# Three edits around the raw loads of a fused RWKV-7 and mixture kernel: R first, loads ahead of the placement, products on GpSimd

## The chip, the cores and the metric

The kernel runs on one core of a Trainium2 chip. The metric is the device time in microseconds (us) of one execution; before the change the median of three runs is 1277.89 us. TensorE multiplies matrices, VectorE (DVE in the profile) and ScalarE (ACT)[...], GpSimd (POOL) works in SBUF, and SyncE (SP) issues most of the DMAs.

## The reference, cut to what matters

Two blocks follow each other. The first is a recurrence with a state matrix for each batch and head (4 batches, 8 heads, 768 steps, 40 columns):

```python
for t in range(S):
    y[:, :, t] = einsum('bhd,bhde->bhe', r_t, state)
    Sa = einsum('bhde,bhe->bhd', state, a_t)
    state = state * w_t - einsum('bhd,bhe->bhde', Sa, b_t) + einsum('bhd,bhe->bhde', v_t, k_t)
```

Its output, laid out as x with 3072 rows of 320, goes through four experts, each 320 to 1024 to 320 columns, weighted by normalized probabilities:

```python
p = domain_probs / (domain_probs.sum(-1) + 1e-9)
for e in range(4):
    out += p[:, e] * (maximum(x @ w1[e], 0) @ w2[e])
```

## The kernel before

The recurrence is cut into chunks of 64 steps. A unit is one chunk of a pair of batches, so there are 24 units, two for each of the 12 chunks. For a unit the kernel does four things.

- `within(q)` works without the state. It loads raw w, transposes it by channels into G and makes G the running product of the decays (a scan); rG is its reciprocal. A, B, K, V and R come as raw tiles from HBM (rawA and so on, one buffer each), are transposed 32 by 32 on VectorE (L229) and become AT, NT, KT, VT and RT. AT is multiplied by G, NT and KT by rG: these are the decay products (L423). A first group of matmuls, pc, multiplies RT with VT; a second, pfe, multiplies AT with NT and KT and gives F (copied by ScalarE) and ET.
- `substitute(q, eng)` inverts the triangular matrix in F. VectorE prepares M (L529 to L545); from the third unit on, GpSimd then computes Z from M by 16 steps of three instructions each (L554, L567).
- `merge(q)` transposes Z on VectorE into Qc and QTc (L578, L580), GpSimd copies QTc into QT (L586), and the matmuls pY and pQ complete QT.
- `step(q, xT)` carries the state: matmuls prn, psat, pxr and pdy with evictions on ScalarE and VectorE (EV, SN, SaT, SX, RS), then Y and the new state. From the third chunk on, twelve DMAs on the SyncE queue place Y into xT (L718, "the placement").

The experts run on the xT of a finished chunk as pieces in a list, `todo`. The product with w2 uses a Strassen-like scheme: `up` multiplies by w1 into two banks ph (L733, L741), ScalarE applies relu into hs, VectorE forms the sums a1, a7, a5, a2, a6 of hs (L842), `down_1` computes p431, `down_2` p75 and p26 (L848), and VectorE adds them to osb (L757, L759). The weights w1 stream through two buffers (w1p); ph, p431, p75 and p26 share three PSUM buffers of the tag "mm".

The main loop takes one unit u in an iteration and weaves stages of four units: the step of u, the merge of u+1, `within` and `substitute` of u+2 and the first loads of u+3. Generators are advanced by `run(gen, n)`; `gap(n)` lets `mix` put in one or two mixture pieces. The raw loads of u+3 are not issued at once but kept in the list `later`; `begin_later(n)` issues the next n of them after each piece, and the rest at once in the next iteration:

```python
        run(s)
        ...
        begin_later(len(later))
        run(w, 1)
        if not early:
            run(m, 1)
        gap(1)
```

Here the third `run(s)` issues the placement of Y, `run(w, 1)` transposes A, B, K, V and R and forms the products, and the first `run(m, 1)` of the merge transposes Z into Qc and QTc. In the early iterations (u below 5) the merge stands elsewhere.

A scheduler turns this program into one fixed order for each engine. `tc.keep_in_program_order` pins an instruction; the loads of `begin_later`, the transposes of M and of Z and the QT copies are pinned, the decay products of later units and the placement are not. Each engine works through its own queue in the resulting order and waits at semaphores.

Of the kernel before, what the change touches and what calls it, by code (L numbers as in the profile page):

```python
# [9 lines left out]
ALU = mybir.AluOpType  # L10
# [5 lines left out]
def kernel(  # L16
# [38 lines left out]
    nc = tc.nc  # L55
# [16 lines left out]
    def big(name):  # L72
# [6 lines left out]
        out=ident[:], in_=ident[:], pattern=[[1, P]], compare_op=ALU.is_equal, fill=0.0,  # L79
# [5 lines left out]
    for t, n, op in ((upf, L, ALU.is_gt), (diagf, Q, ALU.is_equal)):  # L85
        nc.vector.memset(t[:], 1.0)
        for q in range(P // n):
            o = slice(q * n, (q + 1) * n)
            nc.gpsimd.affine_select(
                out=t[o], in_=t[o], pattern=[[1, n]], compare_op=op, fill=0.0, base=0, channel_multiplier=-1,  # L90
# [63 lines left out]
    PADDED = 3  # L154
# [21 lines left out]
    units = []  # L176

    def begin(u):
        q = Unit()
        q.u, q.c, q.bp = u, u // (B // 2), u % (B // 2)  # L180
        q.b = [2 * q.bp, 2 * q.bp + 1]
        q.start, q.end = q.c == 0, q.c == NC - 1
        q.n = {}
        units.append(q)
        return q

    def load(q, names):
        for x in names:
            q.n[x] = t = sb.tile([P, H, D], FP32, name=f"nat{x}", tag=f"nat{x}", bufs=2 if x == "V" else 1)
            for i, bb in enumerate(q.b):  # L190
                nc.sync.dma_start(
                    out=t[i * L:(i + 1) * L], in_=srcs[x][bb, :, q.c * L:(q.c + 1) * L, :].rearrange("h t e -> t h e"),
                )

    def load_raw(q, names):


        moves = []
        for x in names:
            q.n["raw" + x] = t = raw[x]()  # L200
            heads = srcs[x].rearrange("b h t e -> (b h) t e")[q.b[0] * H:(q.b[1] + 1) * H, q.c * L:(q.c + 1) * L, :]
            heads = heads.rearrange("n (x two) e -> x n (two e)", two=2)
            for r in range(2):
                hs = slice(r, 16, 2)
                for y, los, w_ in ((0, (0,), D + Q), (1, (0, D) if x == "W" else (0,), D - Q if x == "W" else 2 * D - Q)):
                    o = slice(64 * r + Q * y, 64 * r + Q * y + Q)
                    for lo in los:
                        cols = slice(Q * y + lo, Q * y + lo + w_)
                        moves.append(
                            lambda eng, out=t[o, :, lo:lo + w_], in_=heads[:, hs, cols]: eng.dma_start(out=out, in_=in_)  # L210
                        )
        return moves
# [10 lines left out]
    def go(moves, eng=None):  # L223
        for move in moves:
            move(eng or nc.sync)

    def turn_raw(out, t):

        return nc.vector.transpose(  # L229
            out=out.rearrange("p n (x two) -> p n two x", two=2),  # L230
            in_=bass.AP(t.tensor, t.offset, [list(t.ap[0]), list(t.ap[1]), [D, 2], [1, Q]]),
        )
# [152 lines left out]
    def within(q):  # L385

        n = q.n

        def pin(ins, also=False):
            if q.u <= PADDED or also:  # L390
                tc.keep_in_program_order(ins)
# [5 lines left out]
        for i in range(2):  # L397
# [5 lines left out]
            out=G[:, 0:2 * NJ * L], data0=G[:, 0:2 * NJ * L],  # L403
# [5 lines left out]
        def turn_padded(x):  # L409
            return turn(f"p{x}T", tok(padded[min(q.u, 1)][x]), q.u == 1)[:].rearrange("p (j i t) -> p j i t", i=2, t=L)  # L410

        def by_channels(name, buf, n_bufs, x, factor=None):

            t = sb.tile([P, 2 * NJ, L], FP32, name=name, tag=buf, bufs=n_bufs)
            to = t[:].rearrange("p (i j) t -> p j i t", i=2)
            if q.u < PADDED:
                src = turn_padded(x)
            else:
                pin(turn_raw(t[:], n["raw" + x][:]))
                src = to  # L420
            if factor is not None:
                factor = factor.rearrange("p (j i) t -> p j i t", i=2)
                pin(nc.vector.tensor_tensor(out=to, in0=src, in1=factor, op=ALU.mult))  # L423
            elif q.u < PADDED:
                nc.scalar.copy(out=to, in_=src)
            return t
# [146 lines left out]
    def merge(q):  # L573


        Qc = sb.tile([P, H, Q], FP32, name="Qc", tag="q", bufs=2)
        QTc = sb.tile([P, H, Q], FP32, name="QTc", tag="q", bufs=2)
        tc.keep_in_program_order(nc.vector.transpose(out=dealt(Qc[:]), in_=q.Z))  # L578
        tc.keep_in_program_order(
            nc.vector.transpose(  # L580
                out=QTc[:].rearrange("p h r -> p (h r)"), in_=Qc[:].rearrange("p h c -> p (h c)"),
            )
        )
        q.QT = QTs()
        for i in range(P // Q):
            ins = nc.gpsimd.tensor_copy(out=q.QT[quarter(i), :, quarter(i % 2)], in_=QTc[quarter(i)])  # L586
            tc.keep_in_program_order(ins)
        yield

        py = big("pY")  # L590
        for h in range(H):
            for i in (1, 3):
                nc.tensor.matmul(
                    out=py[quarter(i - 1), h * Q:(h + 1) * Q], lhsT=q.F[quarter(i), h, 0:Q],
                    rhs=QTc[quarter(i), h, :], start=True, stop=True,
                )
        Y = sb.tile([P, H, Q], FP32, name="Yq")
        for i in (0, 2):
            nc.scalar.copy(out=Y[quarter(i)].rearrange("p h t -> p (h t)"), in_=py[quarter(i), 0:H * Q])
        yield  # L600

        pq = big("pQ")
        for h in range(H):
            for i in (0, 2):
                nc.tensor.matmul(  # L605
                    out=pq[quarter(i), h * Q:(h + 1) * Q], lhsT=Qc[quarter(i), h, :],
                    rhs=Y[quarter(i), h, :], start=True, stop=True,
                )
        for i in (0, 2):
            nc.scalar.copy(out=q.QT[quarter(i), :, quarter(1)], in_=by(pq[quarter(i), 0:H * Q], Q))  # L610
        yield
# [296 lines left out]
    todo, last, later = [], [], []  # L908

    def begin_later(n):  # L910
        for move in later[:n]:
            tc.keep_in_program_order(move(nc.sync))
        del later[:n]

    def mix(n):

        for piece in todo[:n]:
            piece()
            begin_later(3 if n > 1 else 6)
        del todo[:n]  # L920

    def run(gen, n=99):
        if gen is None:
            return
        for _ in range(n):
            if next(gen, gen) is gen:
                break
# [3 lines left out]
    def begin_step(u):  # L931
        q = units[u]
        if q.bp == 0:
            chunks_x[q.c] = sb.tile([P, 3, 2 * P], FP32, name="xT", tag="xT", bufs=2)
        q.xT = chunks_x[q.c][:, :, q.bp * P:(q.bp + 1) * P]
        return step(q, q.xT)
# [79 lines left out]
    for u in range(1, NU):  # L1016
        q = units[u]
        m = s_next = w = w_next = iter(())
        if u + 1 < NU:
            m, s_next = merge(units[u + 1]), begin_step(u + 1)  # L1020
            w_next = ws[u + 1]
        if u + 2 < NU:
            w = ws[u + 2]

        def gap(n, pieces=None):
            at = 4 * u + n
            run(sum_ops, sums_at.get(at, 0))
            mix((1 if at in sparse else 2) if pieces is None else pieces)

        run(w, 1)  # L1030
        run(w_next)
        run(s, 1)
        gap(0)


        early = u < 5
        run(s, 1)
        run(w, 1)
        run(s)
        if u == 1:  # L1040
            mixture_of_unit(q)
        elif q.bp:
            mixture_of_chunk(units[u - 1:u + 1], chunks_x[q.c])
        begin_later(len(later))
        run(w, 1)
        if not early:
            run(m, 1)
        gap(1)

        if u + 3 < NU:  # L1050
            go(load_raw(begin(u + 3), "W"))
            load(units[u + 3], "BKV")
            later.extend(load_raw(units[u + 3], "BAKVR"))
        run(w, 1)
        if early:
            run(m, 1)
        else:
            run(s_next, 1)
            run(m, 1)
        gap(2)  # L1060
# [5 lines that stand above are left out]
            run(s_next, 1)  # L1066
        if u + 2 < NU:
            substitute(units[u + 2], nc.gpsimd)
        run(w, 1)
        if u + 3 < NU:  # L1070
            ws.append(within(units[u + 3]))
            run(ws[u + 3], 1)
        if early:
            run(m, 1)
            run(s_next, 1)
            run(m)
            gap(3, 1)
            run(s_next, 1)
            mix(0 if 4 * u + 3 in sparse else 1)
        else:  # L1080
            gap(3)
        s = s_next
# [31 lines left out]
```

## Time and profile before

| | |
|---|---|
| runs | 1277.89 us median, 1271.62 to 1294.58 |
| profiled span | 1283.8 us |
| granted TensorE clock, mean | 0.887 |
| VectorE decay products L423 of later units | 21 each of AT, NT, KT; 688, 723, 711 ns |
| GpSimd per unit, steady part | 48 instructions of Z, 4 QT copies, 1 copy into Z |
| SyncE placement | 12 issues a unit, 8.9 us |

In the profile a line of the timeline gives start, duration, engine, line, operation, output and inputs, count, and in brackets how long the engine had been idle before it and what released it. A line of waits gives the waiting instruction, the one it waited for, the total, how often and the longest. PEclk shows the granted clock of TensorE in tenths over 40 slices of the span.

### The profile page before, as it was taken

To read this page: it belongs to the slowest core of one execution; us is meant where nothing else is said; L and a number is where in the kernel's file an instruction comes from. 1 tells how busy PE (TensorE), PEld (TensorE's weight loads), DVE (VectorE), ACT (ScalarE), POOL (GpSimd) and SP (SyncE) were. 2 spreads that over 40 slices of the span, in tenths; PEclk is the share of its full clock that TensorE was granted. 3 is DMA by queue.
4 is the path that set the end of the run, shared out by engine and by line. 5 is a ranking of instruction groups with operands and counts; after the bars stand their busy time and mean duration, and the time that the engine had idled before them with its cause. 6 is when DMAs were issued, how large, how long until landed. Compare 5 with 4: busy or idle time off the path is not lost.

```text
span 1283.8 us, 38036 instructions
## 1 busy us (share of the span) xinstructions
PE 1200.6 (94%) x15828; PEld 1045.6 (81%) x15828; DVE 829.7 (65%) x1642; ACT 331.1 (26%) x844; POOL 475.2 (37%) x1226
## 2 busy tenths in 40 slices
PE   5889988999999999999989999999999999999998
PEld 4767766888788888888878888888888887888887
DVE  7865576789656756676566666676666766644334
ACT  2222333223223122232231322322213323122110
POOL 4024555464253351552524515425244253350000
PEclk7789987999797887997979899789797997899999
DMA  7657642445334424443343443442434334212221
GB/s 147 141 135 196 137 91 67 98 101 125 84 99 100 105 74 99 95 114 85 84 109 85 108 104 87 104 99 72 107 86 112 86 104 89 84 57 86 86 76 31
DMA packets 299491, 126.73 MB, mean 99 GB/s; under 512 B 244360, under 2 KB 272696, under 8 KB 299320
## 3 DMA queue, kind: packets, MB, share of 16 engines
q1 hardware_dynamic: 296312, 123.84, 40.5%
q8 instruction: 125, 2.05, 0.7%
q10 hardware_dynamic: 3008, 0.46, 0.2%
q14 instruction: 46, 0.38, 0.1%
HBM read 116.36 MB, written 3.93 MB: 94 GB/s over the span
## 4 chain that ended last, share of the span: by engine, by line
PE 75%; DVE 10%; SPq 7%; DMA 5%; issue 2%; ACT 1%; DVEq 0%; ACTq 0%
PE ph L741 25%; PE p L848 20%; PE ph L733 9%; SPq L718 3%; PE pfe L374 3%; PE pdy L374 2%; PE psat L374 2%; PE prn L374 2%; DMA w1p<-in_moe_w_dram 2%; PE po L782 2%; SPq L210 2%; PE pxr L374 2%; PE pQ L605 2%; DVE osb L759 2%; PE pc L374 1%
## 5 line engine op out<-in xcount | busy, mean ns | idle before, releaser
L741 PE MATMUL ph<-xT,w1p 128*128 128x256 f32 (+1 forms) x1520 | 370.1, 400 | 0.0
L741 PEld LDWEIGHTS ph<-xT,w1p 128*128 128x128 f32 x1520 | 293.3, 203 | 74.6 <-issue 26.3
L567 POOL TENSOR_TENSOR Z<-Z 128x31 f32<-128x31 f32 (+7 forms) x704 | 256.9, 365 | 55.2
L554 POOL TENSOR_TENSOR Z<-M,Z 128x62 f32<-128x62 f32 (+7 forms) x352 | 156.0, 443 | 294.9 <-DVE M L545 258.6
L842 DVE TENSOR_TENSOR a<-hs 128x512 f32<-128x512 f32 x220 | 152.5, 710 | 145.6 <-ACT hs L746 145.6
L746 ACT ACTIVATE hs<-ph 128x512 f32<-128x512 f32 (+1 forms) x208 | 117.2, 564 | 439.9 <-PE ph L741 439.6
L759 DVE SCALAR_TENSOR_TENSOR osb<-p,gate,osb 128x320 f32<-128x320 f32 (+1 forms) x243 | 108.1, 480 | 128.6 <-PE p L848 125.1
L848 PE MATMUL p<-sums,a 128*128 128x160 f32 x1056 | 164.8, 299 | 0.0
L586 POOL COPY QT<-QTc 32x256 f32<-32x256 f32 x96 | 40.1, 418 | 326.7 <-DVE QTc L580 309.1
L848 PEld LDWEIGHTS p<-sums,a 128*128 128x128 f32 x1056 | 152.9, 190 | 2.2
L733 PE MATMUL ph<-xT,w1p 64*128 64x256 f32 (+1 forms) x760 | 138.1, 442 | 0.6 <-ACT xT L710 0.6
L848 PE MATMUL p<-w,hs 128*128 128x160 f32 x704 | 104.2, 301 | 0.0
L848 PE MATMUL p<-w,a 128*128 128x160 f32 x704 | 102.8, 299 | 0.0
L848 PEld LDWEIGHTS p<-w,hs 128*128 128x128 f32 x704 | 100.8, 191 | 2.3
L848 PEld LDWEIGHTS p<-w,a 128*128 128x128 f32 x704 | 98.0, 190 | 0.0
L733 PEld LDWEIGHTS ph<-xT,w1p 64*128 64x128 f32 x760 | 79.5, 207 | 20.1 <-issue 6.3
L439 DVE RECIPROCAL rG<-G 128x504 f32<-128x504 f32 x24 | 79.1, 3296 | 0.0
L634 ACT COPY SN<-prn 64x256 f32<-64x256 f32 x88 | 32.2, 366 | 159.0 <-DVE EV L630 156.6
L529 DVE STREAM_TRANSPOSE M<-blocks 128x1024 f32<-128x1024 f32 x24 | 46.3, 1931 | 35.4 <-ACT blocks L526 35.1
L374 PE MATMUL pc<-RT,VT 40*64 40x64 f32 x768 | 21.2, 264 | 40.4 <-DVE RT L229 39.0
L374 PEld LDWEIGHTS pc<-RT,VT 40*64 40x64 f32 x768 | 17.3, 168 | 46.7 <-DVE RT L229 43.6
L374 PE MATMUL pdy<-VC,k_tok 64*64 64x104 f32 (+1 forms) x768 | 43.6, 269 | 0.0
(153 smaller groups left out, 1489.7 us busy)
## 6 DMA issues: line engine op xcount, KB each, us to landing
w1p<-in_moe_w_dram SPq DMA_DIRECT2D x95, 512.0 KB
w1p<-in_moe_w_dram SPq DMA_DIRECT2D x190, 64.0 KB
w<-in_moe_w_dram SPq DMA_DIRECT2D x4, 1280.0 KB
sums<-in_moe_w_dram SPq DMA_DIRECT2D x9, 512.0 KB
out_dram<-osb SPq DMA_DIRECT2D x46, 80.0 KB
rawW<-in_w_dram SPq DMA_DIRECT2D x47, 72.0 KB
natB<-in_b_dram SPq DMA_DIRECT2D x42, 80.0 KB
natK<-in_k_dram SPq DMA_DIRECT2D x42, 80.0 KB
```

Of the source, the lines that this page charges most:

```text
L374: nc.tensor.matmul(out=p[row][half(col), lo + at * out_cols:lo + (at + 1) * out_cols], lhsT=lhsT, rhs=rhs, start=(n == 0), stop=(n == len( ...
L439: pin(nc.vector.reciprocal(out=rG[:, :, 0:L - 1], in_=Gv[:, :, 1:L]))
L529: ins = nc.vector.transpose(out=M[:], in_=cols)
L554: ins = eng.tensor_tensor(out=Z[:, 1:3, 0:n, j + 1:Q], in0=M[:, j:j + 2, None, j + 1:Q].to_broadcast([P, 2, n, m]), in1=Z[:, here, 0:n, j: ...
L567: eng.tensor_tensor(out=z[:, 0], in0=z[:, 0], in1=z[:, x], op=ALU.add)
L586: ins = nc.gpsimd.tensor_copy(out=q.QT[quarter(i), :, quarter(i % 2)], in_=QTc[quarter(i)])
L733: nc.tensor.matmul(out=ph[i][:, f, :], lhsT=w1.last[i * DT:(i + 1) * DT, f, :], rhs=xT[i * DT:(i + 1) * DT, 2, :], start=(f == 0), stop=False,
L741: nc.tensor.matmul(out=ph[i][:, f, :], lhsT=w1.main[:, g, at * P:(at + 1) * P], rhs=xT[:, g, :], start=False, stop=(g == 1 and f == HF // ...
L746: nc.scalar.activation(out=h[:, i * HF // 2:(i + 1) * HF // 2, 0:n], in_=ph[i][:], func=ACTF.Relu,)
L759: nc.vector.scalar_tensor_tensor(out=to, in0=p, scalar=sc, in1=to, op0=ALU.mult, op1=ALU.add)
L842: nc.vector.tensor_tensor(out=t[:], in0=x, in1=y, op=op)
L848: nc.tensor.matmul(out=p[:, n * HD:(n + 1) * HD], lhsT=a[:, f, :], rhs=b[:, f, :], start=(f == 0), stop=(f == HF - 1),)
```

## The change

It has three parts. The raw loads of a unit come in the order R, B, A, K, V, four for each piece of mixture instead of three, and the remainder is issued before the step's last stages, hence before the placement of Y, so that R isn't the last to arrive. The products of A, B and K with the decays go to GpSimd for every unit from the fourth on. And the order of the later iterations begins at u = 4 instead of 5.

```diff
-                pin(nc.vector.tensor_tensor(out=to, in0=src, in1=factor, op=ALU.mult))
+                pin((nc.vector if q.u < PADDED else nc.gpsimd).tensor_tensor(out=to, in0=src, in1=factor, op=ALU.mult))
...
-            begin_later(3 if n > 1 else 6)
+            begin_later(4 if n > 1 else 6)
...
-        early = u < 5
+        early = u < 4
         run(s, 1)
         run(w, 1)
+        begin_later(len(later))
         run(s)
         if u == 1:
             mixture_of_unit(q)
         elif q.bp:
             mixture_of_chunk(units[u - 1:u + 1], chunks_x[q.c])
-        begin_later(len(later))
         run(w, 1)
...
-            later.extend(load_raw(units[u + 3], "BAKVR"))
+            later.extend(load_raw(units[u + 3], "RBAKV"))
```

## The prediction

> **What bounds the kernel now.** I read the busy shares first, then the list of who waited for whom on TensorE, then the timelines of a steady unit, then the clock in stretches.
>
> ```profile
> PE 1200.6 (94%) x15828; PEld 1045.6 (81%) x15828; DVE 829.7 (65%) x1642; ACT 331.1 (26%) x844; POOL 475.2 (37%) x1226
>
> PE pc L374 <- DVE RT L229: 39.0, 18, 3.2
> PE pev L374 <- DVE ET L381: 13.0, 3, 6.2
> 545.00 0.70 DVE L229 STREAM_TRANSPOSE RT<-rawR 128x512 f32<-128x512 f32 x1
> 545.76 1.09 PE L374 MATMUL pc<-RT,VT 40*64 40x64 f32 x32 [2.16 <-DVE RT L229]
> 538.03 0.97 SPq L210 DMA_DIRECT2D rawR<-in_r_dram  x2
> ```
>
> TensorE is the bound. Its one repeated idle gap is 2.16 us before pc, waiting for RT: R's last two raw loads stand on SyncE behind twelve xT placements (8.93 us) and RT is transposed late on VectorE. The clock pays more than the gap:
>
> ```profile
> 281.68:286.00 4.32, 4.32 (x138) 3.98 (x139) 4.29 (x9) 0.73 (x2) 3.03 (x5) 1.00 0.54 159
> 493.70:498.75 5.05, 5.05 (x135) 4.04 (x136) 4.31 (x11) 2.19 (x6) 1.97 (x5) 0.60 0.67 107
> ```
>
> The columns are stretch, length, busy time of PE, PEld, DVE, ACT, POOL, then granted clock. After the 1.20 us gap at 281.68 the clock stayed 1.00; after the 2.16 us gaps it fell to 0.50. In stretches of 1 us the low episodes last 4 to 18 us, most of them 14 to 18, and lose 7.06 us of clock per unit on average.
>
> A unit of the steady part, from the end of pfe to the end of the next, at full clock and without gaps, from rows at clock 1.00: psat 1.0; four ph blocks of 4.71 (L733 1.06, L741 3.65), 18.84; two p431 of 3.26, 6.52; two p75 with p26 of 4.35, 8.70; pev 0.6, pxr 0.95, pdy 1.74, pg 0.59, pc 0.55, prn 1.05, pY 0.62, pQ 0.62, pfe 1.0. Sum 42.8. With the gap 2.16 and the clock 7.06: 52.0. From pc at 387.95 to pc at 1115.52 are 14 units of 51.97. So the account closes.
>
> GpSimd solves one unit's triangular system, Z:
>
> ```profile
> 510.76 0.29 POOL L554 TENSOR_TENSOR Z<-M,Z 128x62 f32<-128x62 f32 x1 [13.82 <-DVE M L545]
> 532.50 0.52 POOL L567 TENSOR_TENSOR Z<-Z 128x8 f32<-128x8 f32 x2
> 545.63 0.58 DVE L578 STREAM_TRANSPOSE Qc<-Z 128x256 f32<-128x256 f32 x1
> 1152.05 0.63 DVE L578 STREAM_TRANSPOSE Qc<-Z 128x256 f32<-128x256 f32 x1 [3.52 <-POOL Z L567]
> ```
>
> Z takes 22.3 us from M (L545); its only reader, Qc, comes 12.6 us after it ended, so it's hidden. Only in the last unit does Qc stand near: VectorE then sat 3.52 us. This is the wait to watch.
>
> **What the Trainium skill says.** "TensorE: Matmul & The Clock Gate", Part 1: idling drops the array to half clock, and sustained work of some 3.4 us lifts it. The 0.50 agrees; but here 2.16 us of idling beside small matmuls is enough, and once dense work is back (503.95) it takes 5 us. The same page, under the array's architectural detail: VectorE's queue is strict FIFO. The 3.52 us agree: everything behind Qc waited too. "GPSIMD Engine Reference", section 3.1: a two-input tensor_tensor of 2048 elements takes 4497 ns. No 128x512 product on GpSimd is in this trace; this gives 1.12 us for 512, an estimate. L554's fastest, 0.23 us at 16 elements and 0.45 at 152, extrapolate to 1.03; section 8's sharing of SBUF interfaces with VectorE shows as L567 going from 217 to 1246 ns. I take 1.2 and bound it at 1.0 and 2.0.
>
> **The change part by part.**
> Products to GpSimd: 63 of them leave VectorE (15.2 + 14.4 + 14.9 = 44.5 us, 2.1 a unit). They add 3 x 1.2 = 3.6 us a unit to GpSimd (2.0 each: 6), behind Z and ahead of the QT copies, where it idles 13.81 us. Readers are pfe for NT and KT, prn for AT. Hidden, both ends.
> R first, raw loads ahead of the placement, four loads in place of three a piece: the same DMAs. R lands early, the 2.16 us gap closes. V becomes last but no longer waits for 8.93 us of placement issues.
> Later order one unit sooner: iteration 4 alone, about nothing.
>
> What the diff doesn't show is where these put Qc. In the order of the changed program, VectorE's queue has, in every second unit (call it E):
>
> ```
> L545 M<-M,Z          (Z may start)
> L759 osb<-p431 x4
> L381 SX<-pxr x2
> L229 RT<-rawR
> L578 Qc<-Z           (waits for all of Z)
> L580 QTc<-Qc
> L842 a1, a7;  L759 osb<-p75;  L842 a5;  L759 osb<-p75
> ```
>
> Qc is 8 rows after M; in the kernel before 46. In the other units (O) it is 22 rows after. E and O alternate from the eighth to the 23rd unit: eight pairs. Queued behind Qc are a1, a7 and the osb additions that read p75; the second ph bank of the next up-projection waits on TensorE for exactly the last of these, since it takes p75's PSUM buffer.
>
> Unit E, clock zero at the end of pfe. VectorE: F at 0.8, ET 0.43, blocks 0.57, ET 0.40, G's four instructions and scan 2.5 (4.8); M transposed 1.93, gl 0.17, the reciprocal 3.3, which now stands ahead, 0.17, then 0.69 + 0.69: M ends at 11.8. Z: 0.35 to start, and 19.5 to run (fastest of every form and its gaps add up to 18.9; VectorE, idle, disturbs little): 31.7. Qc 0.6, QTc 0.45, a1 and a7 1.4, osb 0.55, a5 0.68, osb 0.37: 35.9. TensorE: psat 1.0, ph 4.7, p431 3.26, pev and pxr 1.55, ph 4.7, p75 and p26 4.35, pdy and pg 2.3: at 22.0 it's out of work. **Stall 13.9 us.** Later pc waits for VT, behind the next a1, barely; then VectorE reaches VC and EV late, SN and Yq on ScalarE follow (1.5 + 0.75), and pQ stands 2.2 us.
>
> Unit O: M ends near 6.8 (the reciprocal now after it), Z at 28.7 with contention. Here p75's buffer is free at 25.3, so Qc costs TensorE some 0.8. But pg needs rG, at 14.7, where TensorE is free at 10.6: 4.1 us.
>
> Clock: the old episode at pc goes with its gap. In E the restart after 13.9 us costs about 3 (half of the 5 to 7 us for which dense work ran slow before), the stand at pQ perhaps 3; in O the stand at pg about 3.
>
> E: 42.8 + 13.9 + 2.2 + 6 = 64.9. O: 42.8 + 4.1 + 0.8 + 3 = 50.7. A pair 115.6 against 103.9: +11.7, eight pairs +93. Units six and seven (Qc 13 and 17 rows after M) and iteration 4 gain the gap and part of the clock and lose some of it at Qc: -5. 1278 + 93 - 5 = **1366 us**.
>
> **The rivals.**
> A, faster: Qc doesn't hold VectorE up, and gap and clock episode go. For it: the 2.16 us gap is aimed at precisely, and the unit after 281.68 ran at 1.00 throughout. Full effect 18 x (2.16 + 7.06) = 166, 1112 us; with the clock falling at the small matmuls anyway, 18 x 2.16, 1239. Against: the 22 us of Z don't fit into the 3.1 us of VectorE work (osb 1.6, SX 0.78, RT 0.7) between M and Qc.
> B, stall but little clock loss: only 3 us of slow clock in a pair, no stand at pQ: pair 42.8 x 2 + 13.9 + 4.9 + 3 = 107.4, +28 over eight, 1301 us. If TensorE's stand were 4 us shorter too, nearly no change. For it: no episode has been seen after a stall amid dense work.
> C, stall with long episodes: 7 us more at pQ and at pg as at pc before, 3 at the restart: pair 123.7, +158, 1431. For it: pQ and pg stand beside the same small matmuls as pc did.
> D, GpSimd becomes the bound: 22 + 6 + 2 us of a unit of 50 is not enough.
>
> **How the numbers follow.** Forecast 0.55, B 0.17, C 0.17, A 0.08, D 0.03 (near 1400). A is almost all faster; a third of B is within 2%. So faster 0.06, same 0.05, slower 0.89. The range reaches from B to just short of C: 1300 to 1420.
>
> **What would show it.** Right: VectorE idle on Qc waiting for POOL Z for about 16 us in every second unit from the eighth on (some 130 us in all); TensorE's ph L733 waiting for VectorE osb for about 14 us as often; the RT wait before pc gone; PE busy under 90%; L423 on POOL between 1.0 and 2.0 us. Wrong: Qc following Z without idle time, units below 52 us, or pc waiting for VT as long as it did for RT.

## The result, and the profile after

The changed kernel takes 1341.75 us (median of three runs, 1341.01 to 1345.63), against 1277.89 before. All ratios here are taken against the kernel before timed beside each run, and leave out the executions that ran in a slower state, so they differ a little from the ratio of two medians. This one is 1.053 with a 95% interval of 1.046 to 1.061: 5.3% slower. The profiled span is 1343.8 us against 1283.8, the mean granted clock 0.907 against 0.887. So the profiled execution is 60 us longer although TensorE's mean clock got better.

First the page of the changed kernel: the busy shares, the engines' shares of the chain that ended last, and two groups of instructions (count, then busy time and mean ns of one, then the idle time of the engine just before them and who ended most of it).

```profile
PE 1156.7 (86%) x15828; PEld 1002.8 (75%) x15828; DVE 786.1 (58%) x1579; ACT 331.0 (25%) x844; POOL 514.1 (38%) x1289
...
PE 53%; DVE 17%; issue 8%; POOL 7%; SPq 7%; DMA 5%; ACT 2%; DVEq 0%; ACTq 0%; POOLq 0%
...
L578 DVE STREAM_TRANSPOSE Qc<-Z 128x256 f32<-128x256 f32 x24 | 14.9, 619 | 175.0 <-POOL Z L567 174.8
...
L423 POOL TENSOR_TENSOR NT<-NT,rG 128x512 f32<-128x512 f32 x21 | 26.9, 1283 | 77.1 <-DVE NT L229 77.1
```

TensorE went from 94% to 86% busy, and its share of the chain from 75% to 53%. VectorE does less work than before (786.1 us against 829.7), as it should with 63 products gone, and still sits 174.8 us in front of 24 transposes of 0.62 us each. Idle time of an engine off the bound costs nothing; whether this one costs is told by TensorE's own waits (total, times, longest):

```profile
PE ph L733 <- issue: 93.6, 10, 12.2
PE pg L341 <- DVE rG L440: 21.2, 7, 4.0
...
PE p L848 <- DVE osb L759: 11.0, 2, 6.7
...
PE pc L374 <- DVE VT L229: 5.4, 1, 5.4
```

The wait for RT before pc, 39.0 us in 18 before, is gone; one wait for VT of 5.4 is what is left there. In its place ph stands 93.6 us. "issue" means that the trace shows no releaser. The timelines of one unit give it, the twelfth; VectorE first:

```profile
541.52 0.69 DVE L545 TENSOR_TENSOR M<-M,Z 128x512 f32<-128x512 f32 x1
542.13 1.58 DVE L759 SCALAR_TENSOR_TENSOR osb<-p,gate,osb 128x320 f32<-128x320 f32 x4
543.63 0.77 DVE L381 COPY_PREDICATED SX<-mask_up,pxr 128x256 f32<-128x256 int32 x2
544.29 0.71 DVE L229 STREAM_TRANSPOSE RT<-rawR 128x512 f32<-128x512 f32 x1
561.45 0.61 DVE L578 STREAM_TRANSPOSE Qc<-Z 128x256 f32<-128x256 f32 x1 [16.46 <-POOL Z L567]
562.10 0.45 DVE L580 STREAM_TRANSPOSE QTc<-Qc 128x256 f32<-128x256 f32 x1
562.47 1.25 DVE L842 TENSOR_TENSOR a<-hs 128x512 f32<-128x512 f32 x2
563.64 0.55 DVE L759 SCALAR_TENSOR_TENSOR osb<-p,gate,osb 128x320 f32<-128x320 f32 x1
564.10 0.68 DVE L842 TENSOR_TENSOR a<-hs 128x512 f32<-128x512 f32 x1
564.70 0.38 DVE L759 SCALAR_TENSOR_TENSOR osb<-p,minus_gate,osb 128x160 f32<-128x160 f32 x1
```

```profile
553.55 0.70 PE L733 MATMUL ph<-xT,w1p 64*128 64x256 f32 x2
565.18 2.04 PE L733 MATMUL ph<-xT,w1p 64*128 64x256 f32 x6 [10.93 <-issue]
```

The transposes stand right behind M, RT the last of them, and Qc comes next in the queue. The row of Qc is 0.61 us of work behind 16.46 us of waiting, because Z, which began at 542.36, ran until 561.4 on GpSimd. The osb additions behind Qc read p75. The last ends at 565.08, and 0.10 us later TensorE goes on with a ph that takes p75's buffer; in the built program this matmul waits for exactly that addition. The releaser that the trace left out is read from the end time of the other engine's row.

TensorE's stand is 10.93 and not 16.46 us, because it still had work until 554.25. How the loss lies in a pair of units is seen in the windows of the same kernel (stretch, length, busy PE, PEld, DVE, ACT, POOL with counts, then clock and DMA): a unit of kind E, one of kind O, then six pairs.

```profile
542.40:597.30 54.90, 43.02 (x546) 37.17 (x545) 26.69 (x57) 12.77 (x31) 21.02 (x56) 0.88 0.40 96
597.30:650.60 53.30, 49.87 (x775) 43.67 (x773) 37.98 (x73) 14.54 (x39) 24.17 (x56) 0.97 0.39 91
436.10:1088.80 652.70, 559.33 (x7937) 487.29 (x7930) 387.66 (x769) 164.81 (x421) 269.89 (x673) 0.91 0.39 91
```

TensorE is idle for 54.90 - 43.02 = 11.9 us of the first stretch and for 3.4 of the second; a pair takes 652.70 / 6 = 108.8 us, where before it took 103.9. Laying the trace's records of the granted clock over TensorE's rows splits a pair in three: 15.6 us idle (4.7 before), 5.4 us of clock lost while at work (12.8 before), and 87.8 us of work at full clock (86.4 before). So the change does win back clock, 7.4 us a pair, and loses more than that to the stands.

### The profile page after: what moved, and what is told of

Same layout as the page of the kernel before. It is cut to its first block, busy times and chain, and to the rows that moved or that the text cites. A ratio compares the mean times of both kernels' runs of the same rounds, so it can differ in the third digit from the quotient of the medians.

```text
span 1343.8 us, 38059 instructions
## 1 busy us (share of the span) xinstructions
PE 1156.7 (86%) x15828; PEld 1002.8 (75%) x15828; DVE 786.1 (58%) x1579; ACT 331.0 (25%) x844; POOL 514.1 (38%) x1289
## 4 chain that ended last, share of the span: by engine, by line
PE 53%; DVE 17%; issue 8%; POOL 7%; SPq 7%; DMA 5%; ACT 2%; DVEq 0%; ACTq 0%; POOLq 0%
PE ph L741 19%; PE p L848 16%; PE ph L733 6%; POOL Z L567 5%; SPq L718 3%; POOL Z L554 3%; PE po L782 3%; DVE rG L439 3%; PE pdy L374 3%; DMA w1p<-in_moe_w_dram 2%; SPq L210 2%; DVE osb L759 2%; DVE a L842 2%; DVE M L529 1%; DVE G L402 1%
## 5 line engine op out<-in xcount | busy, mean ns | idle before, releaser
L554 POOL TENSOR_TENSOR Z<-M,Z 128x62 f32<-128x62 f32 (+7 forms) x352 | 137.1, 390 | 396.1 <-DVE M L545 363.6
L842 DVE TENSOR_TENSOR a<-hs 128x512 f32<-128x512 f32 x220 | 160.4, 739 | 194.8 <-ACT hs L746 185.3
L567 POOL TENSOR_TENSOR Z<-Z 128x31 f32<-128x31 f32 (+7 forms) x704 | 232.7, 331 | 55.2
L733 PE MATMUL ph<-xT,w1p 64*128 64x256 f32 (+1 forms) x760 | 129.4, 438 | 94.4 <-issue 93.6
L848 PE MATMUL p<-sums,a 128*128 128x160 f32 x1056 | 168.0, 303 | 4.4 <-DVE osb L759 4.3
L578 DVE STREAM_TRANSPOSE Qc<-Z 128x256 f32<-128x256 f32 x24 | 14.9, 619 | 175.0 <-POOL Z L567 174.8
L848 PE MATMUL p<-w,a 128*128 128x160 f32 x704 | 106.3, 302 | 3.3 <-ACT hs L746 3.3
L423 POOL TENSOR_TENSOR NT<-NT,rG 128x512 f32<-128x512 f32 x21 | 26.9, 1283 | 77.1 <-DVE NT L229 77.1
L423 POOL TENSOR_TENSOR AT<-AT,G 128x512 f32<-128x512 f32 x21 | 27.0, 1286 | 68.8 <-DVE AT L229 60.0
```

The source lines that it names most:

```text
L423: pin((nc.vector if q.u < PADDED else nc.gpsimd).tensor_tensor(out=to, in0=src, in1=factor, op=ALU.mult))
L554: ins = eng.tensor_tensor(out=Z[:, 1:3, 0:n, j + 1:Q], in0=M[:, j:j + 2, None, j + 1:Q].to_broadcast([P, 2, n, m]), in1=Z[:, here, 0:n, j: ...
L567: eng.tensor_tensor(out=z[:, 0], in0=z[:, 0], in1=z[:, x], op=ALU.add)
L733: nc.tensor.matmul(out=ph[i][:, f, :], lhsT=w1.last[i * DT:(i + 1) * DT, f, :], rhs=xT[i * DT:(i + 1) * DT, 2, :], start=(f == 0), stop=False,
L842: nc.vector.tensor_tensor(out=t[:], in0=x, in1=y, op=op)
L848: nc.tensor.matmul(out=p[:, n * HD:(n + 1) * HD], lhsT=a[:, f, :], rhs=b[:, f, :], start=(f == 0), stop=(f == HF - 1),)
```

## The experiments

The theory: Qc's place on VectorE, 8 rows behind M, makes the loss. Rivals: the load order in itself, GpSimd's new products, and the loads that now go ahead of the placement.

Why does Qc stand there at all? `keep_in_program_order` pins an instruction behind the one traced just before it on the same engine, and the one traced just before Qc is the last transpose of `turn_rv`: RT. RT itself isn't pinned. The built orders, in which rows of VectorE between M and Qc can be counted from the eighth unit on, show how Qc goes with RT. Three of these programs were built and not run: the later order alone, four loads a piece alone, and all but R first.

| built program | rows from M to Qc |
|---|---|
| before | 46 |
| products on GpSimd alone | 43 |
| later order one unit sooner, alone | 46 |
| loads ahead of the placement alone | 51 to 53 |
| four loads a piece alone | 34 and 44 or 45 |
| R first alone | 8 |
| all of it (the change) | 8 and 22 |
| all but R first | 31 and 42 |
| all, RT traced ahead of VT | 31 and 42 |

Once R arrives first, the scheduler takes RT early, and Qc, which can only follow RT, comes with it. The last row suggests the mildest repair: let VT be traced last, so that Qc hangs on VT.

**Run 1: all of the change, RT ahead of VT.**

```diff
         def turn_rv():
-            VT = by_channels("VT", "turned", 3, "V")
+            if q.u < PADDED:
+                VT = by_channels("VT", "turned", 3, "V")
             q.RT = by_channels("RT", "RT", 2, "R")
+            if q.u >= PADDED:
+                VT = by_channels("VT", "turned", 3, "V")
             return VT
```

> The changed kernel with one thing more: RT is transposed before VT in the program, so that Qc, which is pinned behind the transpose traced before it, stands behind VT (31 or 41 rows after M) and not behind RT (8 or 22). Theory (Qc in front of unfinished Z stops VectorE and then TensorE): VectorE's idle time on Qc falls from 175 us to under 25, TensorE's stand before ph L733 from 94 us to under 10, and the time drops below that of the kernel before, to 1130 to 1220 us, since the gap before pc is closed as well. Rival (the products on GpSimd slow the unit down, by sharing SBUF with VectorE or by standing before the QT copies): still 1300 us or more.

Measured: 1215.54 us, ratio to the kernel before 0.949 (0.944 to 0.953), a hit. The same loads, products and merge, with two transposes exchanged, take 126 us less. Four loads a piece, the loads ahead of the placement and the later order are all still there, so none of them makes the loss. In its VectorE timeline Qc follows VT with no idle time:

```profile
522.24 0.70 DVE L229 STREAM_TRANSPOSE VT<-rawV 128x512 f32<-128x512 f32 x1
522.87 0.57 DVE L581 STREAM_TRANSPOSE Qc<-Z 128x256 f32<-128x256 f32 x1
```

VectorE's whole idle time at Qc is 6.7 us. TensorE's waits in run 1:

```profile
PE pg L341 <- DVE rG L443: 23.5, 8, 4.0
...
PE pc L374 <- DVE VT L229: 8.7, 7, 5.0
...
PE ph L736 <- issue: 1.4, 2, 1.0
```

The wait of ph is gone and pg's is now the largest. The clock lost over the whole span, in stands and at work, is 63.2 us from stretches of 1 us, against 145.5 before and 124.8 in the changed kernel. This is what the change was for, and Qc had hidden it.

**Run 2: the kernel before with R first, and nothing else.**

```diff
-            later.extend(load_raw(units[u + 3], "BAKVR"))
+            later.extend(load_raw(units[u + 3], "RBAKV"))
```

> The kernel before with the raw loads in the order R, B, A, K, V and nothing else. Its built order has Qc 8 rows after M in every unit from the eighth on. Theory: the stall comes with this edit alone and in every unit, not in every second: Qc idles VectorE about 16 us in each of 16 units, 250 us or more in all, and the time is 1350 to 1420 us. Rival (it is the GpSimd products): within 2% of the kernel before.

Measured: 1451.51 us, 1.129 (1.119 to 1.139), above the time that was expected. One letter's place in a string costs more than the whole change. Two views, VectorE's and TensorE's waits:

```profile
DVE Qc L578 <- POOL Z L567: 233.9, 18, 16.5
```

```profile
PE ph L733 <- issue: 127.5, 18, 11.0
PE pc L374 <- DVE VT L229: 39.6, 18, 3.3
```

Every steady unit pays now, not each second one. And the old wait before pc isn't even gone: V, now last, stands behind the placement as R did, and VT comes late (39.0 us in 18 waits for RT before, 39.6 in 18 for VT here).

**Run 3: the kernel before with the products on GpSimd, and nothing else.**

```diff
-                pin(nc.vector.tensor_tensor(out=to, in0=src, in1=factor, op=ALU.mult))
+                pin((nc.vector if q.u < PADDED else nc.gpsimd).tensor_tensor(out=to, in0=src, in1=factor, op=ALU.mult))
```

> The kernel before with the products of A, B and K on GpSimd and nothing else; Qc stays 43 rows after M. Theory: hidden, within 1% of the kernel before, the gap before pc still about 2 us; L423 on POOL 1.27 us. Rival (products on GpSimd are the cost): 1330 us or more.

Measured: 1289.79 us, 1.007 (1.003 to 1.011), within the expected 1%; pc still waits for RT, 41.1 us in 18, and VectorE sits at Qc for 3.2 us in the whole kernel.

**Run 4: all of the change but the products, which stay on VectorE.**

```diff
-                pin((nc.vector if q.u < PADDED else nc.gpsimd).tensor_tensor(out=to, in0=src, in1=factor, op=ALU.mult))
+                pin(nc.vector.tensor_tensor(out=to, in0=src, in1=factor, op=ALU.mult))
```

> The changed kernel with the products of A, B and K on VectorE again; Qc stays 8 and 21 rows after M. Theory: as slow as the changed kernel, 1320 to 1365 us, VectorE idle on Qc for 150 to 180 us. Rival: back at 1280 us or below.

Measured: 1340.07 us, 1.046 (1.042 to 1.050); the changed kernel took 1341.75. TensorE's ph waits 92.8 us in 8 and VectorE's Qc 176.2 us, nearly what they are with the products moved. So GpSimd's products aren't the cause: without them the loss is nearly all there, and alone they cost 0.7% (run 3).

**Run 5: run 1 with pg pinned to its place in the program,** to remove the largest wait of run 1.

```diff
-            pg = by(turn("pg", tok(rG))[:], 64)[:, :, 0:D]
+            pg = by(turn("pg", tok(rG), q.u > PADDED)[:], 64)[:, :, 0:D]
```

> The run with RT before VT, and pg's first transpose pinned on TensorE behind the matmul traced before it; in the built order pg then stands behind pdy in both units of a pair, where rG is long ready. Theory: the waits pg for rG (23.5 us in that run) and the half-clock episodes that follow them (about 3.4 us of clock each, six of them) go: 1175 to 1195 us. Rival (the wait only moves to another place, or the clock falls anyway at the small matmuls): 1205 to 1215 us.

Measured: 1219.66 us, 0.952 (0.945 to 0.960): a miss, and the rival was right. The wait moved to the next instruction that VectorE serves behind the same reciprocal:

```profile
PE pdy L374 <- DVE SX L381: 30.8, 11, 4.2
```

**Run 6: run 5 with the products on VectorE.** The edit is that of run 4.

> The same as the run with pg pinned, but the products of A, B and K stay on VectorE. Theory: VectorE, at 65% busy, has room for 44 us more and TensorE is the bound, so within 1.5% of that run. Rival (with the stall gone VectorE is what TensorE waits for, and the products on GpSimd pay): 2% or more slower than that run.

Measured: 1206.23 us (1205.13 to 1206.71), 0.943 (0.936 to 0.949). This is the lowest median of all, 1.1% below run 5, whose times (1213.43 to 1220.49) don't overlap with it. VectorE has slack for the products, and without them it is disturbed less: the sums a (L845) take 706 ns on average here and 750 in run 5, the longest 946 and 1767. That this makes the 1.1% isn't shown, and runs 9 and 10 don't repeat it.

**Run 7: the kernel before with the remainder of the loads ahead of the placement, and nothing else.**

```diff
         run(w, 1)
+        begin_later(len(later))
         run(s)
         if u == 1:
             mixture_of_unit(q)
         elif q.bp:
             mixture_of_chunk(units[u - 1:u + 1], chunks_x[q.c])
-        begin_later(len(later))
```

> The kernel before with the rest of the raw loads issued before the placement and nothing else; R is still last, Qc stands 51 to 53 rows after M, RT right before it. Theory: no wait on Z; R lands some 9 us earlier, so the part of the gap before pc that was landing goes, but RT's place on VectorE behind the sums and additions stays: the gap stays at 0.5 to 2 us and the time within 2% of the kernel before or up to 4% faster. Rival (the gap came from the landing alone): gap under 0.5 us, no clock episodes, 1150 to 1200 us.

Measured: 1281.53 us, 1.000 (0.997 to 1.002). The time is as expected, the reason isn't: the gap before pc didn't shrink but became 2.19 and 3.69 us in turn.

```profile
PE pc L374 <- DVE RT L229: 48.4, 17, 3.7
PE pQ L605 <- ACT Yq L599: 25.6, 18, 3.4
```

R is issued ahead of the placement, and RT is late all the same. So the placement on SyncE wasn't the whole reason of the old gap. VectorE's order is the likely other one; run 11 looks at it.

**Run 8: run 2 with RT ahead of VT,** that is R first, with Qc hung on VT (the edits of runs 1 and 2).

> The kernel before with the loads in the order R, B, A, K, V and RT transposed before VT, nothing else; Qc stands 46 rows after M again. Theory (it was Qc's place, not the load order itself, that cost the 12.9% of R first alone): no wait on Z; V now takes R's place behind the placement, so pc waits for VT as it did for RT: within 2% of the kernel before. Rival (R first has another cost): over 3% slower.

Measured: 1283.65 us, 1.002 (0.998 to 1.005), while run 2 took 1451.51. The load order is the same in both. So it was Qc's place, not the load order, that cost the 12.9%. What R gains at pc is given back by V: pc waits 39.6 us in 18 for VT.

**Runs 9 and 10: run 1 with the reciprocal of G moved** from the start of the iteration behind SX and pinned there, since runs 1 and 5 showed the waits of pg and SX behind it. Run 9 has the products on VectorE, run 10 on GpSimd.

```diff
-        pin(nc.vector.reciprocal(out=rG[:, :, 0:L - 1], in_=Gv[:, :, 1:L]))
+        pin(nc.vector.reciprocal(out=rG[:, :, 0:L - 1], in_=Gv[:, :, 1:L]), q.u >= 6)
...
-        run(w, 1)
+        if u < 4:
+            run(w, 1)
...
-        run(w, 1)
+        run(w, 1 if early else 2)
```

> RT before VT, products on VectorE, and the reciprocal of G (3.3 us on VectorE) traced after SX and pinned there from the seventh unit on, in place of pg's pin. In the built order SX no longer stands behind it. Theory (in the run with pg pinned the wait moved from rG to SX because both stood behind this reciprocal): the waits of pg and pdy, 33.5 us, and most of the half-clock episodes beside them, 25 us of clock, go: 1145 to 1175 us. Rival (a third wait takes their place, or the episodes come from the small matmuls): 1190 us or more.

> The same with the products of A, B and K on GpSimd. If the products cost about 1% as they did in the runs before (1.0066 alone, 1219.7 against 1206.2 us with pg pinned), this is 8 to 20 us slower than its twin. If that was chance, within 5 us of it.

Measured: 1207.50 us (the median of 1203.04, 1207.50 and 1215.68; a fourth execution, at 2741.09, is left out), 0.943 (0.934 to 0.953), and 1209.34 us, 0.945 (0.936 to 0.953). Run 9 misses its range, and its rival was right: both are within 1% of run 1. The profile of run 9 is of the execution left out and isn't used. In run 10 TensorE's waits are

```profile
PE pg L341 <- DVE rG L442: 30.9, 18, 4.1
...
PE pdy L374 <- DVE SX L381: 8.8, 11, 1.3
```

SX came nearly free (30.8 us in run 5), and pg pays in every unit. In both places where the 3.30 us of the reciprocal were put, something that TensorE needs soon stands behind them. On the products the two runs say nothing: they differ by 1.8 us, less than their own spread.

**Runs 11 and 12: what carries the gain of run 1?** Loads ahead (run 7) and R first with RT ahead of VT (run 8) had brought nothing one by one. Run 11 puts the two together; run 12 adds four loads a piece to run 11. Both keep the products on VectorE and the later order from the sixth unit.

```diff
-            begin_later(3 if n > 1 else 6)
+            begin_later(4 if n > 1 else 6)
```

> The kernel before with R loaded first, RT transposed ahead of VT (so that Qc stays behind VT) and the remainder of the raw loads issued ahead of the placement; three loads a piece, products on VectorE, later order from the sixth unit. Loads ahead alone and R first with VT behind RT were each within 0.2% of the kernel before. If the two belong together (the tile that arrives last must neither stand behind the placement nor be transposed late), pc waits for VT under 15 us in all, as in the kernel with RT ahead of VT (8.7 us), and the time is 1200 to 1230 us. Rival: VectorE's place of VT is what counts, late in both, and the arrival of V does not matter; then pc waits for VT some 40 us in 18 and the time is 1270 to 1290 us; the gain then hangs on four loads for each piece.

> The same with four raw loads for each piece in place of three; the products still on VectorE, later order still from the sixth unit. If the pair of R first and loads ahead carries the gain, within 1% of the run with three loads a piece. Rival: four loads a piece are what closes the gap before pc; then this one takes 1200 to 1230 us and the other stays near 1280 us.

Measured: run 11 took 1293.71 us, 1.008 (1.005 to 1.010), run 12 1214.54 us, 0.947 (0.939 to 0.954). The rival was right: the pair brings nothing (it is 0.8% slower), and the digit 4 on top of it brings 6%. The waits of TensorE in run 11, then in run 12:

```profile
PE pc L374 <- DVE VT L229: 58.2, 17, 4.3
PE pQ L608 <- ACT Yq L602: 25.0, 18, 3.4
```

```profile
PE pg L341 <- DVE rG L443: 33.8, 9, 4.0
...
PE pc L374 <- DVE VT L229: 6.9, 2, 3.7
```

In run 11 the last load of V was issued at 530.2, and VT ran at 547.49, with VectorE not idle before it: the data wasn't what VT waited for, its place in the queue was. With four a piece the built order puts Qc, and VT right before it, 34 and 44 or 45 rows behind M instead of 51 and 53, and pc nearly always finds VT ready. Run 12 is equal to run 1 within 0.1%, so the products and the later order one unit sooner add nothing that these runs can tell. Whether loads ahead are needed beside four a piece, and what four a piece would do alone, was not run.

## Why the prediction was right, point by point

Direction and mechanism came as forecast, and 1341.75 lies in the range, 24 us below the 1366. That near hit is in part luck: two wrong terms partly cancel. Between the kernels' starts of Z, the change was 22.0 us behind at the eighth unit (325.8 against 303.8) and 60.9 at the last (1191.6 against 1130.7); the tail gave back 0.9. So the eight pairs cost 39 us where the forecast had 93, and the units before them 22 where it had a gain of 5.

- **The bound and the wait to watch.** Right: the 3.52 us that VectorE sat at Qc in the last unit of before became 16.4 to 16.5 in every second unit, as forecast, and 174.8 in all.
- **The skill's places.** That VectorE's queue is strict FIFO ("TensorE: Matmul & The Clock Gate", the array's architectural detail) carries the whole result; at 544.99 nothing behind Qc moved for 16.46 us. The price from "GPSIMD Engine Reference", section 3.1, scaled to 1.12 us and taken as 1.2, measured 1.27 (median) with a least of 1.25: inside the bounds, a little above the estimate. One reading in support was wrong: L567 going from 217 to 1246 ns compares instructions of 8 elements with others of 29. Those of 29 alone run from 244 to 1246 ns in the kernel before, so that they are disturbed at times holds.
- **Products to GpSimd, hidden.** Right for the change: run 4 moves the time by 1.7 us. Not quite free in general: 0.7% in run 3, 1.1% between runs 5 and 6. Missing in the argument was that they slow VectorE's own rows (last section).
- **The stall of E, 13.9 us.** It measured 10.7 to 11.4 in the six middle pairs, 11.1 on average. In the unit shown above, counted from the end of pfe: M ended at 10.9 (forecast 11.8), Z ran 19.06 us (19.5), p75's buffer was free at 33.8 (35.9), and TensorE ran out at 22.9 (22.0). Each step is near; the two ends moved towards each other by 3 us.
- **pQ, 2.2 us; pg, 4.1; Qc in O, 0.8; clock, 9.** They measured 0.8, 2.9, about 0 and 5.4. The clock was low for 18.8 us of a pair, but 7.9 of them fell into TensorE's stands, where a low clock costs nothing.
- **The pair, +11.7 us: the term that was too large.** It measured +4.9 (108.8 against 103.9), hence +39 and not +93 over eight pairs. TensorE's stands come to 15.6 us of a pair and not 21.0, its clock loss to 5.4 and not 9, and its work at full clock to 87.8 and not 85.6; what these 2.2 are was not traced. A small difference of two large sums takes all these errors in. The account of a unit before closed in the same way, with errors that cancel: 43.2 of work, 2.4 idle and 6.4 of clock, where the forecast has 42.8, 2.16 and 7.06.
- **The early units, -5: the step that failed.** They cost +22. Units six and seven were taken for a gain, because Qc stands 13 and 17 rows behind M there. But VectorE was through with these rows long before Z was done, and sat 13.42 us at Qc in the sixth and 10.97 in the seventh (at 293.50):

```profile
237.88 0.63 DVE L578 STREAM_TRANSPOSE Qc<-Z 128x256 f32<-128x256 f32 x1 [13.42 <-POOL Z L567]
```

Behind it TensorE stood 4.33 us at 244.33 and 6.71 at 295.48, both before p for osb. From the sixth unit's start of Z to the eighth's the change took 109.0 us against 90.6: 11.7 more of TensorE idle, 4.6 more of clock lost at work, 2.2 more of work. The remaining 3.6 of the 22 were lost before that, 2.2 of them where pc waited 5.41 us for VT (at 207.72) in place of 3.24 for RT. The same arithmetic as for E, done for these two units, would have shown their stall.
- **Rivals.** A (the gap and its clock episodes go) was a true account of what the loads are worth, blocked by Qc: run 12 takes 1214.54, between A's 1112 and 1239. The forecast gave four loads a piece no price ("the same DMAs"); in run 12 it is what decides. The clock loss of 5.4 us a pair lies between B's 3 and C's 17. D is out, POOL was 38% busy.

## What to carry to other kernels

In a queue that works in order, an instruction that waits for a slow engine belongs where the slow engine is done, so when the arrival of a load changes, ask which waiting instruction is anchored to the one that reads it. Before a change is judged, undo its side effect on the order and time it again: here two transposes exchanged turned 5.3% slower into 5.1% faster. Parts that look alike on paper (an order of loads, how many in one go) are worth a run each and then together: R first and the loads ahead brought nothing, one by one or as a pair, and with four in one go added the three brought 5.4%.

## What the runs showed of the hardware that wasn't expected

- The length of a gap alone doesn't tell what the clock does. Of the 16 gaps of 2.16 us before pc in the kernel before, beside small matmuls, 13 were followed by 14 to 17 us of low clock. Of eight stands of 2.66 to 2.87 us before pg in run 10, amid the wide matmuls of the experts, two were followed by low clock, for 3.4 us each. That the small matmuls make the difference isn't shown.
- In all the profiles used here an episode of low clock lasted 3.4 us or a multiple of it (6.8, 10.2, 13.7, 17.1 and so on), but for the last one, which the end of the profile cuts. "TensorE: Matmul & The Clock Gate", Part 1, has sustained work of about 3.4 us lift the clock. After the eight stands of 10.7 to 12.2 us before ph in the changed kernel, dense work ran at 0.50 for 3.5 to 6.7 us more, which agrees, and cost 1.8 to 3.4 us of clock. After the stand shown above (stretch, length, busy PE, PEld, DVE, ACT, POOL, clock, DMA):

```profile
565.18:568.60 3.42, 3.42 (x10) 2.35 (x11) 3.42 (x6) 0.00 (x0) 1.27 (x1) 0.50 0.21 48
```

- Z on GpSimd takes 19.06 us where VectorE waits for it, and 21.2 to 21.6 in the O units of the changed kernel, where VectorE works (22.3 to 22.8 in the steady units before). The other way round, the 159 VectorE sums (L842) beside no GpSimd work of the changed kernel took 0.64 to 0.69 us, the 48 beside Z up to 0.89, and ten of the 13 beside a product 1.60 to 1.79. "GPSIMD Engine Reference", section 8, names the SBUF interfaces that GpSimd shares with VectorE, with contention where a VectorE instruction has two SBUF inputs; the sum has two. That page gives no size for it. In the changed kernel, VectorE and then GpSimd:

```profile
566.65 1.61 DVE L842 TENSOR_TENSOR a<-hs 128x512 f32<-128x512 f32 x1
```

```profile
566.44 1.27 POOL L423 TENSOR_TENSOR NT<-NT,rG 128x512 f32<-128x512 f32 x1 [5.02 <-DVE NT L229]
```
